# Chunked attention and two expert layers on one core: wider conversion steps, scales finished from PSUM, later maxima

## The chip, the cores and the metric

The kernel runs on one core of one Trainium2 chip. The metric is the device time of one execution in microseconds (us). The kernel before took 1036.71 us, the median of three runs (1036.70, 1036.71 and 1039.64).

A core has TensorE (PE, matmuls; PEld is its weight load), VectorE (DVE), ScalarE (ACT), GpSimd (POOL) and SyncE (SP, which issues the transfers here).

## The reference

Three layers follow each other. All inputs are float32.

- Attention in chunks of 64: 8 batches, 8 heads, 576 positions, head dimension 64. In each chunk `softmax(q k^T / 8) v`. The result is 4608 rows of 512.
- `h = max(x @ w_in, 0)`, then `(h * h) @ w_out`, with w_in 512 x 2048 and w_out 2048 x 512.
- A soft mixture: `logits = x @ phi` (32 slots), one softmax over all 4608 rows, which mixes the rows into 32 slot inputs; eight experts of four slots each (`max(s @ w1, 0) @ w2`); one softmax over the slots, which mixes the slot outputs back into 4608 rows.

w_in and w_out arrive as 8-byte floats and are turned into 4-byte floats on the core.

## The kernel before, in words

The rows are worked in 36 tiles of 128 (two batches, one chunk). Blocks of tiles are one, two and then three tiles each. For each block and each of 16 pieces f of the hidden dimension there is one step: `moe_h` (L752, PE, twelve matmuls), relu with a scale (L776, or L778 on DVE), square (L783, L785), a rounded copy gh (L175) and its remainder gl (L795), and `moe_out` (L813 to L815, PE, three matmuls per tile). All matmuls use parts: a rounded high part and a low part that holds what the rounding lost.

A conversion `conv(f)` makes piece f of both weight matrices. Two loads of 512 KB bring the 8-byte words. ACT takes their upper 16 bits and makes a clamped float of them (`up`, L277). DVE joins exponent and mantissa (`join`) with three instructions per matrix of 128x512: L289, L290, L294. Then DVE takes w_in's absolute maximum (`total`, L169), PE spreads it over the partitions with a matmul against ones (`reduce`, L192), and DVE finishes a power-of-two scale and its inverse in four small instructions, L200, L201, L202 and L205 (`finish`). ACT rounds w_in's piece with that scale (`hi`, L177), DVE makes the remainder (`lo`, L329), ACT or POOL rounds w_out's piece (`whi`, L175 or L184) and POOL makes its remainder (`wlo`, L339).

Attention tiles 0 to 6 are worked in float32 (`attention32`), 7 to 35 in 16-bit parts (`attention`). Both take maxima (L169) and finish scales by the same four small instructions. For a 16-bit tile ACT rounds q and k (L410), DVE makes the remainders (L415, and L430 for v), and a transfer transposes them (L436).

Order. The conversions, tiles 0 to 8 and the steps of the first three blocks form a list. A planner (`list_schedule`) writes it: each operation has engines that can do it, a duration on each, operations that it depends on, and a rank; at each point the planner takes what can start first, and of those that can start within AHEAD of it the one of lowest rank. HOP is the time that it allows from an operation's end to one that depends on it, and SLACK shifts the choice of engine. The list is then issued in exactly this order on all engines. PARTS tells how many f the first blocks do before the next ones start: with (8, 11), blocks 0 and 1 do f 0 to 7 as steps of 128 and of 256 columns, block 2 does f 0 to 10, then blocks 0 and 1 together do f 8 to 15 as steps of 384 columns, and block 2 the rest.

Code behind the list (blocks 3 to 12, the soft mixture) is ordered by the framework, which can move an instruction ahead into the list where its own model of the engines has a hole. The maxima of w_out, 16 instructions that the code issues with the steps of block 3, are such instructions.

Buffers. Conversions have four sets of load buffers, used in turn. The intermediate values of `up` and `join` lie in buffers that tile 8 uses later (qk16 and p16 of even tiles); the first copies of tile 8 wait for the last join.

Of the kernel before, what the change touches and what calls it, by code (L numbers as in the profile page):

```python
# [39 lines left out]
class Op:  # L40
# [8 lines left out]

    def __call__(self):  # L50
        self.fn(self.eng) if self.choose else self.fn()


def cost_of(kind, n):

    return {
        "read": {"act": 0.23 + 0.00088 * n, "dve": 0.08 + 0.00105 * n},
        "scaled": {"act": 0.26 + 0.00092 * n, "dve": 0.08 + 0.00105 * n},
        "copy": {"act": 0.2 + 0.00083 * n, "dve": 0.1 + 0.0007 * n, "pool": 0.2 + 0.0011 * n},
        "two": {"dve": 0.07 + 0.00105 * n, "pool": 0.2 + 0.0021 * n},  # L60
        "square": {
            "act": 0.2 + 0.00083 * n, "dve": 0.07 + 0.00105 * n, "pool": 0.2 + 0.0021 * n,
        },
    }[kind]
# [7 lines left out]
def kernel(  # L72
# [47 lines left out]
    two = const.tile([P, 2], F32, name="two")  # L120
    one, least = two[:1, 0:1], two[:, 1:2]
# [67 lines left out]
    def pow2_scale(am, n):  # L189

        ps = misc()[:, :n]
        pe.matmul(ps, ones, am, start=True, stop=True)  # L192
        return ps

    def pow2_finish(ps, n, tag, bufs, inv=None):
        gm = sm.tile([P, n], F32, tag=tag + "g", name=tag + "g", bufs=2)
# [11 lines left out]
        return s, inv  # L208
# [29 lines left out]
    def conv(f):  # L238
# [30 lines left out]
        def upper(a, eng):  # L269


            h = raws[a].bitcast(I16)[:, 4 : 4 + 2048].rearrange("p (n t) -> p n t", t=4)[:, :, 0]
            v[a] = qk16_b[(N32 + 1) % 2].rearrange("p a n -> p (a n)").bitcast(F32)[
                :, 512 * a : 512 * a + 512
            ]
            if eng == "act":
                act.activation(out=v[a], in_=h, func=ACTF.Relu, scale=2.0 ** 19, bias=least)  # L277
            else:
                (dve if eng == "dve" else pool).tensor_scalar(
                    v[a], h, -LEAST, 2.0 ** 19, ALU.max, ALU.mult  # L280
                )
            v["off", a] = LEAST if eng == "act" else 0.0

        def join(a):


            m = p16_b[(N32 + 1) % 2].rearrange("p a n -> p (a n)").bitcast(F32)
            s, off = 2.0 ** 19, v["off", a]
            dve.tensor_scalar(m, v[a], (14336.0 + off) * s, -2 * off * s, ALU.max, ALU.add)  # L289
# [4 lines left out]
            dve.scalar_tensor_tensor(  # L294
                out=word(a), in0=word(a), scalar=13, in1=m.bitcast(I32),
                op0=ALU.logical_shift_right, op1=ALU.bitwise_or,
            )

        for a in range(2):
            deps = [(("f", x), n) for x in before for n in ("lo", "wlo", "hi", "whi")]  # L300
            ops[f"load{a}"] = Op("dma", 2.4, deps, 0, lambda a=a: load(a))
        for a in range(2):
            last = [(("f", f - 1), f"join{a}")] if f else []
            ops[f"up{a}"] = Op(
                {"act": 0.72, "dve": 0.65, "pool": 1.5}, None, [f"load{a}", *last], 1 + a,
                lambda e, a=a: upper(a, e),
            )
            ops[f"join{a}"] = Op("dve", 1.65, [f"up{a}"], 1 + a, lambda a=a: join(a))
# [62 lines left out]
    def attention(i):  # L371
# [23 lines left out]
        def finish():  # L395
            v["s"], inv = pow2_finish(v["gm"], 3, "a", 5)
            v["iv"] = inv[:, 2:3]
            if not normed:
                pool.tensor_tensor(
                    out=iv2_all[:, i : i + 1], in0=v["iv"], in1=v["iv"], op=ALU.mult  # L400
                )
            v["es"] = sm.tile([P, 1], F32, tag="es", name="es", bufs=4)
            dve.scalar_tensor_tensor(
                out=v["es"], in0=inv[:, 0:1], scalar=scale, in1=inv[:, 1:2],
                op0=ALU.mult, op1=ALU.mult,
            )
# [111 lines left out]
        def xscale():  # L518
            v["xs"], inv = norm_finish(v["xn"], "x", 4, 77 + 127, 127 - 77)
            dve.scalar_tensor_tensor(  # L520
                out=inv, in0=inv, scalar=1.0 / PSH, in1=v["iv"], op0=ALU.mult, op1=ALU.mult
            )
# [32 lines left out]
        ops["finish"] = Op("dve", 0.6, ["reduce"], 1, finish)  # L555
# [5 lines left out]
        conv_end = [(("f", NF - 1), f"join{a}") for a in range(2)] if i == N32 + 1 else []  # L561
# [17 lines left out]
        ops["sums"] = Op("dve", 0.85, ["exp"], 7, sums)  # L579
# [10 lines left out]
        ops["xl"] = Op("dve", 0.6, ["xh"], 12, xl)  # L590
        return ops

    def attention32(i):
# [20 lines left out]
        def finish():  # L614
            v["s"], inv = pow2_finish(v["gm"], 1, "a32", 5)
            pool.tensor_tensor(out=iv2_all[:, i : i + 1], in0=inv, in1=inv, op=ALU.mult)
# [100 lines left out]
        ops["sums"] = Op("dve", 0.85, ["exp"], 4, sums)  # L717
# [99 lines left out]
    def scales16():  # L817


        nonlocal kappa, beta  # L820
        m = sm.tile([P, 2], BF16, tag="m16", name="m16", bufs=1)
        dve.tensor_reduce(out=m[:, 0:1], in_=wi_max, axis=AX.X, op=ALU.max)
        dve.tensor_reduce(out=m[:, 1:2], in_=wo_max, axis=AX.X, op=ALU.max)
        ps = misc()
        norm_scale(ps[:, 0:1], m[:, 0:1])
        pe.matmul(ps[:, 1:2], ones, m[:, 1:2], start=True, stop=True)
# [6 lines left out]
        dve.tensor_scalar_mul(act_w, inv_w, alpha)  # L833
# [365 lines left out]
    pool.memset(ones, 1.0)  # L1199
# [45 lines left out]
    def list_schedule():  # L1245
        free = {"pe": 3.0, "dve": 3.0, "act": 2.5, "pool": 5.0, "dma": 0.7}
# [7 lines left out]
        def add(task, ops, rank):  # L1254
            for x, (n, op) in enumerate(ops.items()):
                me = (task, n)
                deps = [d if isinstance(d, tuple) else (task, d) for d in op.deps]
# [3 lines left out]
                for d in deps:  # L1261
                    if d not in end:
                        missing[me] += 1
                        after.setdefault(d, []).append((me, op, rank + 0.01 * x))
                if not missing[me]:
                    for e in op.on:
                        avail[e][me] = (rank + 0.01 * x, op)
# [64 lines left out]
        while ph < len(left) or left_s or any(avail.values()):  # L1332
# [56 lines left out]
            fin_ = t + op.on[op.eng]  # L1389
            free[op.eng] = fin_  # L1390
# [80 lines left out]
    while t < end or any(x >= t for x in slots):  # L1471
# [232 lines left out]
```

## Time and profile before

| | |
|---|---|
| runs (median of 3) | 1036.71 us |
| the profiled execution | 1034.19 us, span 1032.4 us, mean granted clock of TensorE 0.967 |
| PE busy | 962.5 us, 93% of the span |
| DVE busy | 658.4 us, 64% |
| ACT busy | 546.5 us, 53% |
| POOL busy | 248.9 us, 24% |
| transfers | 112.18 MB, mean 109 GB/s |
| chain that ended last | PE 74%, DVE 12%, DMA 6% |

The span runs from the first to the last instruction; the execution's own time lies a little above it. Busy shares are means over the whole span; what a stretch is bound by has to be read from that stretch. [...] Where a wait has several causes, the profile names the one that came last.

### The profile page before, as it was taken

How to read it: one execution, taken by the hardware profiler on the slowest of the kernel's cores; microseconds unless marked ns; L12 is line 12 of the kernel's file. 1: busy time of each engine (PE TensorE's matmuls, PEld its weight loads, DVE VectorE, ACT ScalarE, POOL GpSimd, SP SyncE). 2: the span in 40 equal slices, each digit the busy share in tenths (PEclk: the TensorE clock that was granted, in tenths of full speed). 3: DMA queues.
4: the chain of work that ended last, by engine and by line, in shares of the span. 5: the costliest groups of instructions: out<-in, count | busy, mean ns of one | idle time of the engine just before them, and what ended most of it. 6: DMA issues, size and time to landing. Idle time of an engine off the chain costs nothing.

```text
span 1032.4 us, 18731 instructions
## 1 busy us (share of the span) xinstructions
PE 962.5 (93%) x7182; PEld 583.8 (57%) x7182; DVE 658.4 (64%) x1469; ACT 546.5 (53%) x1029; POOL 248.9 (24%) x252
## 2 busy tenths in 40 slices
PE   5667998999999999999999999999999999999983
PEld 4555665677666665555555555555555555554442
DVE  6898887746878977667667666566675562123232
ACT  5665765445558665465555555554655644534132
POOL 3463443432313442112122111111121220001100
PEclk8988998999999999999999999999999999999995
DMA  7746352233363374333233334333334451347998
GB/s 158 207 131 205 70 122 93 53 59 74 79 107 62 60 183 105 62 62 62 63 62 73 69 78 84 66 63 63 62 63 63 123 142 33 86 160 223 298 279 240
DMA packets 248618, 112.18 MB, mean 109 GB/s; under 512 B 208080, under 2 KB 241872, under 8 KB 248528
## 3 DMA queue, kind: packets, MB, share of 16 engines
q1 hardware_dynamic: 248528, 110.98, 45.2%
q8 instruction: 56, 0.92, 0.4%
q14 instruction: 34, 0.28, 0.1%
HBM read 78.71 MB, written 9.44 MB: 85 GB/s over the span
## 4 chain that ended last, share of the span: by engine, by line
PE 74%; DVE 12%; DMA 6%; SPq 2%; ACT 2%; issue 2%; POOL 1%; POOLq 0%; DVEq 0%; ACTq 0%
PE hps L752 31%; PE x L815 10%; PE x L813 10%; PE x L814 10%; DVE p L290 2%; PE ehps L1556 2%; PE misc L990 2%; DVE stage L294 2%; PE misc L977 1%; DMA out_dram<-o 1%; DVE p L289 1%; SPq L1627 1%; DMA qkv<-in_k_dram 1%; PE sop L1642 1%; DMA qkv<-in_q_dram 1%
## 5 line engine op out<-in xcount | busy, mean ns | idle before, releaser
L752 PE MATMUL hps<-xb,wi 128*128 128x384 f16 (+2 forms) x2400 | 416.4, 323 | 3.9 <-DVE wi L329 3.9
L752 PEld LDWEIGHTS <-wi 128*128 128x128 f16 x2400 | 225.7, 99 | 173.1 <-issue 27.2
L813 PE MATMUL x<-wo,gh 128*128 128x512 f16 (+1 forms) x576 | 229.1, 398 | 1.9 <-DVE x2sb L878 1.1
L814 PE MATMUL x<-wo,gh 128*128 128x512 f16 (+1 forms) x576 | 223.3, 388 | 0.0
L815 PE MATMUL x<-wo,gl 128*128 128x512 f16 (+1 forms) x576 | 208.5, 390 | 4.2 <-POOL gl L795 2.1
L795 DVE TENSOR_TENSOR gl<-g,gh 128x384 f16<-128x384 f32 (+1 forms) x162 | 99.7, 616 | 110.8 <-ACT gh L175 107.4
L776 ACT ACTIVATE g<-hps,act_w 128x384 f32<-128x384 f32 x128 | 73.9, 578 | 147.0 <-PE hps L752 115.9
L476 POOL TENSOR_TENSOR ex<-ex,rs 128x512 f32<-128x512 f32 x29 | 31.1, 1073 | 383.9 <-DVE rs L473 260.3
L175 ACT ACTIVATE gh<-g 128x384 f16<-128x384 f32 (+3 forms) x196 | 100.0, 511 | 19.5 <-PE x L814 15.8
L783 ACT ACTIVATE g<-g 128x384 f32<-128x384 f32 (+1 forms) x196 | 100.0, 511 | 4.7
L169 DVE TENSOR_REDUCE am<-qkv 128x1 bf16<-128x512 f32 x94 | 63.8, 686 | 48.0 <-DMA qkv<-in_k_dram 20.0
L425 POOL TENSOR_SCALAR vbd<-qkv,as 64x512 f16<-64x512 f32 x58 | 58.6, 1010 | 54.6 <-PE x L815 13.5
L815 PEld LDWEIGHTS <-gl 128*128 128x128 f16 x384 | 37.0, 98 | 44.6 <-DVE gl L795 2.8
L814 PEld LDWEIGHTS <-gh 128*128 128x128 f16 x384 | 37.5, 98 | 36.7 <-issue 1.4
L415 DVE SCALAR_TENSOR_TENSOR qk<-qkv,as,qk 128x512 f16<-128x512 f32 x58 | 54.7, 967 | 5.3 <-ACT qk L410 4.7
L813 PEld LDWEIGHTS <-gh 128*128 128x128 f16 x384 | 37.5, 98 | 36.1 <-issue 0.4
L776 ACT ACTIVATE g<-hps,inv_w 128x384 f32<-128x384 f32 (+1 forms) x70 | 37.5, 537 | 28.8 <-PE hps L752 23.8
L440 DVE COPY qbd<-qkT 64x1024 f16<-64x1024 f16 x58 | 25.6, 441 | 41.5 <-DMA qkT<-qk 41.1
L430 DVE SCALAR_TENSOR_TENSOR vbd<-qkv,as,vbd 64x512 f16<-64x512 f32 x58 | 47.4, 817 | 5.4 <-POOL vbd L425 4.4
L410 ACT ACTIVATE qk<-qkv,as 128x512 f16<-128x512 f32 x58 | 38.5, 712 | 15.8 <-DVE as L202 15.8
L813 PEld LDWEIGHTS x<-wo,gh 128*128 128x128 f32 x192 | 37.1, 193 | 15.9 <-issue 3.7
L795 POOL TENSOR_TENSOR gl<-g,gh 128x384 fp32r<-128x384 f32 (+2 forms) x38 | 36.4, 960 | 35.9 <-ACT gh L175 27.6
(223 smaller groups left out, 1394.1 us busy)
## 6 DMA issues: line engine op xcount, KB each, us to landing
unit<-in_moe_w_dram SPq DMA_DIRECT2D x36, 512.0 KB, 4.2
unit<-in_moe_w_dram SPq DMA_DIRECT2D x56, 256.0 KB, 5.7
qkv<-in_q_dram SPq DMA_DIRECT2D x72, 128.0 KB, 3.4
qkv<-in_k_dram SPq DMA_DIRECT2D x72, 128.0 KB, 3.4
qkv<-in_v_dram SPq DMA_DIRECT2D x72, 128.0 KB, 3.3
stage<-in_moe_w_in_dram SPq DMA_DIRECT2D x16, 512.0 KB, 4.9
stage<-in_moe_w_out_dram SPq DMA_DIRECT2D x16, 512.0 KB, 5.6
out_dram<-o SPq DMA_DIRECT2D x16, 256.0 KB, 4.2
```

The lines of the kernel that those rows point to most:

```text
L169: dve.tensor_reduce(out=am, in_=src, axis=AX.X, op=ALU.max, apply_absolute_value=True)
L175: act.activation(out=out, in_=in_, func=ACTF.Copy)
L415: dve.scalar_tensor_tensor(out=qk16[:, 2 * a + 1], in0=flat[:, a], scalar=v["s"][:, a : a + 1], in1=qk16[:, 2 * a], op0=ALU.mult, op1=ALU. ...
L425: pool.tensor_scalar(out=dst[0], in0=vin, scalar1=v["s"][pr, 2:3], scalar2=1.0, op0=ALU.mult, op1=ALU.mult,)
L430: dve.scalar_tensor_tensor(out=dst[1], in0=vin, scalar=v["s"][pr, 2:3], in1=dst[0], op0=ALU.mult, op1=ALU.subtract,)
L752: pe.matmul(hp, wi[f][:, wl, kt], xb[:, xl, kt, :n], start=(nm == 0), stop=(nm == 3 * KT - 1))
L776: act.activation(out=r["g"], in_=r["hp"], func=ACTF.Relu, scale=sc)
L783: act.activation(out=g, in_=g, func=ACTF.Square)
L795: (dve if eng == "dve" else pool).tensor_tensor(out=r["gl"], in0=r["g"], in1=r["gh"] if parts16(b) else r["gh"].bitcast(F32), op=ALU.subtract,
L813: pe.matmul(o, gh[:, c], w[:, 0], start=first, stop=False)
L814: pe.matmul(o, gh[:, c], w[:, 1], start=False, stop=False)
L815: pe.matmul(o, gl[:, c], w[:, 0], start=False, stop=last)
```

## The change

- `up` runs on ACT only, and writes both matrices into one buffer of 128x1024. `join` becomes one operation: L289's and L290's instructions run once over 1024 columns, L294's stays one per matrix. It waits for both loads. The buffers are now qk16 of both tile parities, so the first copies of tiles 7 and 8 both wait for the last join.
- `pow2_scale` gets a second matmul that adds a tiny constant, and the ones become 2^-13. `pow2_finish` then needs two instructions, both reading PSUM, and no lower bound. The powers of two that this shifts are made good where the scales are used.
- The maxima of w_out become an operation `wmax` of the list. It depends on the last join, and its rank is raised by 200.
- PARTS goes from (8, 11) to (9, 12). The planner has new durations, ranks, HOP, AHEAD and SLACK. A new `share` lengthens some DVE operations in the plan when POOL is busy.

```diff
-PARTS = (8, 11)
+PARTS = (9, 12)
-AHEAD = 0.01
-HOP = 0.15
-SLACK = {'act': 3.5, 'dve': -2.69, 'pool': -0.65}
+AHEAD = 0.2
+HOP = 0.18
+LATER = 200.0
+SLACK = {'act': 0.39, 'dve': -3.6, 'pool': -0.9}
...
-        pe.matmul(ps, ones, am, start=True, stop=True)
+        pe.matmul(ps, ones, am, start=True, stop=False)
+        pe.matmul(ps, ones, tiny[:, :n], start=False, stop=True)
...
-        dve.tensor_scalar_max(gm, ps, 2.0 ** -100)
-        dve.tensor_single_scalar(gm.bitcast(I32), gm.bitcast(I32), 0x7F800000, ALU.bitwise_and)
+        bits = ps.bitcast(I32)
         dve.tensor_scalar(
-            s.bitcast(I32), gm.bitcast(I32), -1.0, float(268 << 23), ALU.mult, ALU.add
+            s.bitcast(I32), bits, 0x7F800000, 0x7F800000, ALU.bitwise_xor, ALU.bitwise_and
         )
-        dve.tensor_scalar(
-            inv.bitcast(I32), gm.bitcast(I32), float(-(14 << 23)), None, ALU.add
-        )
+        dve.tensor_single_scalar(inv.bitcast(I32), bits, 0x7F800000, ALU.bitwise_and)
...
+        def join():
+            u, m, s, off = wide(0), wide(1), 2.0 ** 19, LEAST
+            dve.tensor_scalar(m, u, (14336.0 + off) * s, -2 * off * s, ALU.max, ALU.add)
+            dve.scalar_tensor_tensor(
+                out=m.bitcast(I32), in0=u, scalar=(off - 14336.0) * s, in1=m,
+                op0=ALU.min, op1=ALU.add,
+            )
+            for a in range(2):
+                dve.scalar_tensor_tensor(
+                    out=word(a), in0=word(a), scalar=13,
+                    in1=m.bitcast(I32)[:, 512 * a : 512 * a + 512],
+                    op0=ALU.logical_shift_right, op1=ALU.bitwise_or,
                 )
...
+        last = [(("f", f - 1), "join")] if f else []
         for a in range(2):
+            ops[f"up{a}"] = Op("act", 0.67, [f"load{a}", *last], 1, lambda a=a: upper(a))
+        ops["join"] = Op("dve", 3.3, ["up0", "up1"], 2, join)
...
+        ops["wmax"] = Op(
+            "dve", 0.61, ["whi", (("f", NF - 1), "join")], 6,
+            lambda: largest_of(wo[f][:, 0].bitcast(F32), wo_max[:, f : f + 1]),
+        )
...
-        conv_end = [(("f", NF - 1), f"join{a}") for a in range(2)] if i == N32 + 1 else []
+        conv_end = [(("f", NF - 1), "join")] if i in (N32, N32 + 1) else []
...
+            if op.eng == "dve" and op.share:
+                fin_ += op.share * min(1.0, max(0.0, free["pool"] - t) / op.on["dve"])
...
-            if b == F16_FROM - 2:
-                largest_of(wo[f][:, 0].bitcast(F32), wo_max[:, f : f + 1])
```

The ranks of tiles and conversions (RANK_T, RANK_F, RANK_S), the cost table and the single durations are replaced by new numbers throughout.

## Rows read from the trace of the kernel before

**Rows 1.** Busy us by stretch: PE, PEld, DVE, ACT, POOL; then clock, DMA share, GB/s

```profile
18.00:100.00 82.00, 58.45 (x644) 45.41 (x643) 76.16 (x168) 51.34 (x96) 39.31 (x46) 0.87 0.61 167
100.00:180.00 80.00, 73.27 (x381) 49.61 (x380) 64.84 (x119) 50.46 (x96) 32.57 (x31) 0.95 0.43 105
180.00:232.00 52.00, 52.00 (x380) 36.76 (x379) 32.25 (x58) 25.03 (x46) 18.89 (x19) 1.00 0.30 55
...
340.00:940.00 600.00, 596.20 (x4279) 335.44 (x4278) 365.23 (x858) 320.92 (x603) 113.93 (x100) 1.00 0.38 84
```

**Rows 2.** PE's waits, 18 to 100 us: us in total, times, longest

```profile
PE misc L192 <- DVE wi_max L169: 5.6, 5, 1.7
PE misc L676 <- POOL ex L669: 3.9, 3, 1.9
PE hps L752 <- DVE wi L329: 3.9, 4, 2.2
PE misc L192 <- DVE wg L200: 3.5, 2, 2.9
```

**Rows 3.** PE's waits, 100 to 180 us

```profile
PE misc L192 <- DVE wi_max L169: 6.2, 3, 3.8
```

**Rows 4.** DVE's timeline at 42.66 us: start, us, line, operation

```profile
42.66 0.15 DVE L200 TENSOR_SCALAR wg<-misc 128x1 f32<-128x1 f32 x1
...
43.03 0.15 DVE L202 TENSOR_SCALAR ws<-wg 128x1 int32<-128x1 int32 x1
...
43.16 0.74 DVE L698 SCALAR_TENSOR_TENSOR xb<-misc,a32s,xb 128x512 f16<-128x512 f32 x1
```

**Rows 5.** L200 by stretch: length, DVE busy and count

```profile
18.00:100.00 82.00, 2.07 (x14) 0.87 0.61 167
100.00:180.00 80.00, 1.20 (x8) 0.95 0.43 105
```

**Rows 6.** The maxima of w_out by stretch

```profile
18.00:100.00 82.00, 4.73 (x7) 0.87 0.61 167
100.00:180.00 80.00, 5.45 (x8) 0.95 0.43 105
```

**Rows 7.** L294 by stretch

```profile
18.00:100.00 82.00, 11.67 (x15) 0.87 0.61 167
100.00:180.00 80.00, 11.70 (x16) 0.95 0.43 105
180.00:232.00 52.00, 0.69 (x1) 1.00 0.30 55
```

**Rows 8.** PE's timeline at 346 us

```profile
346.14 0.18 PE L192 MATMUL misc<-am,ones 128*128 128x3 bf16 x1
346.18 4.06 PE L752 MATMUL hps<-xb,wi 128*128 128x384 f16 x24
```

**Rows 9.** The h matmuls by shape, 0 to 330 us: count, busy us, mean ns

```profile
L752 PE MATMUL hps<-xb,wi 128*128 128x384 f16 x576 | 103.2, 331 | 0.0
...
L752 PE MATMUL hps<-xb,wi 128*128 128x256 f16 x96 | 14.4, 311 | 0.0
...
L752 PE MATMUL hps<-xb,wi 128*128 128x128 f16 x96 | 8.2, 234 | 3.9 <-DVE wi L329 3.9
```

**Rows 10.** POOL's and DVE's timelines at 164 us

```profile
164.07 1.17 POOL L795 TENSOR_TENSOR gl<-g,gh 128x384 fp32r<-128x384 f32 x1 [0.38 <-POOL gl L795]
...
164.42 1.37 DVE L290 SCALAR_TENSOR_TENSOR p<-qk,p 128x512 int32<-128x512 f32 x1
...
168.14 0.69 DVE L290 SCALAR_TENSOR_TENSOR p<-qk,p 128x512 int32<-128x512 f32 x1
```

**Rows 11.** L415 of tiles 7 and later, by shape, 0 to 330 us

```profile
L415 DVE SCALAR_TENSOR_TENSOR qk<-qkv,as,qk 128x512 f16<-128x512 f32 x16 | 15.5, 986 | 0.6 <-ACT qk L410 0.5
```

**Rows 12.** Transfers by kind, 0 to 260 us: count, us to landing

```profile
qkT<-qk SPq DMA_TRANSPOSE x4, 5.2
```

**Rows 13.** DVE's timeline at 219 us

```profile
219.49 0.69 DVE L534 SCALAR_TENSOR_TENSOR xb<-misc,xb 128x512 f16<-128x512 f32 x1 [4.29 <-ACT xb L528]
```

More of the change, by code (lines that the diff above doesn't have):

```diff
@@ L48, in __init__ @@
         self.deps, self.stage, self.fn = deps, stage, fn
+        self.share = 0.0
     def __call__(self):
@@ L56, in cost_of @@
     return {
[L57 to L60, printed above, removed]
+        "read": {"act": 0.13 + 0.00092 * n, "dve": 0.08 + 0.00105 * n},
+        "scaled": {"act": 0.27 + 0.00088 * n, "dve": 0.08 + 0.00105 * n},
+        "copy": {"act": 0.12 + 0.0008 * n, "dve": 0.1 + 0.0007 * n, "pool": 0.2 + 0.0013 * n},
+        "two": {"dve": 0.07 + 0.00105 * n, "pool": 0.2 + 0.0023 * n},
         "square": {
-            "act": 0.2 + 0.00083 * n, "dve": 0.07 + 0.00105 * n, "pool": 0.2 + 0.0021 * n,
+            "act": 0.2 + 0.0009 * n, "dve": 0.07 + 0.00105 * n, "pool": 0.2 + 0.0024 * n,
         },
@@ L119 @@
     ones = const.tile([P, P], BF16, name="ones")
-    two = const.tile([P, 2], F32, name="two")
-    one, least = two[:1, 0:1], two[:, 1:2]
+    four = const.tile([P, 4], F32, name="four")
+    one, least, tiny = four[:1, 0:1], four[:, 1:2], four[:, 2:4].bitcast(BF16)
     phi_sb = const.tile([P, KT, NS], F32, name="phi_sb")
@@ L187, in copy, with pow2_scale @@
             )
-    def pow2_scale(am, n):
-        ps = misc()[:, :n]
-        pe.matmul(ps, ones, am, start=True, stop=True)
+    def pow2_scale(am, n, ps=None):
+        ps = misc()[:, :n] if ps is None else ps
+        pe.matmul(ps, ones, am, start=True, stop=False)
+        pe.matmul(ps, ones, tiny[:, :n], start=False, stop=True)
         return ps
     def pow2_finish(ps, n, tag, bufs, inv=None):
-        gm = sm.tile([P, n], F32, tag=tag + "g", name=tag + "g", bufs=2)
         s = sm.tile([P, n], F32, tag=tag + "s", name=tag + "s", bufs=bufs)
@@ L267, in load, with wide, upper @@
             )
-        def upper(a, eng):
+        def wide(x):
+            return qk16_b[x].rearrange("p a n -> p (a n)").bitcast(F32)
+        def upper(a):
             h = raws[a].bitcast(I16)[:, 4 : 4 + 2048].rearrange("p (n t) -> p n t", t=4)[:, :, 0]
[L273 to L280, printed above, removed]
-                )
[L282 to L289, printed above, removed]
+            act.activation(
+                out=wide(0)[:, 512 * a : 512 * a + 512], in_=h, func=ACTF.Relu,
+                scale=2.0 ** 19, bias=least,
+            )
+        def join():
+            u, m, s, off = wide(0), wide(1), 2.0 ** 19, LEAST
+            dve.tensor_scalar(m, u, (14336.0 + off) * s, -2 * off * s, ALU.max, ALU.add)
             dve.scalar_tensor_tensor(
-                out=m.bitcast(I32), in0=v[a], scalar=(off - 14336.0) * s, in1=m,
+                out=m.bitcast(I32), in0=u, scalar=(off - 14336.0) * s, in1=m,
                 op0=ALU.min, op1=ALU.add,
             )
[L294 to L297, printed above, removed]
+            for a in range(2):
[4 more added lines that the diff above has]
+                )
         for a in range(2):
@@ L590, in attention @@
         ops["xl"] = Op("dve", 0.6, ["xh"], 12, xl)
+        for n in ("lo0", "lo1", "vl0", "vl1", "qd0", "qd1", "normal"):
+            ops[n].share = 0.4
         return ops
@@ L825, in scales16 @@
         norm_scale(ps[:, 0:1], m[:, 0:1])
-        pe.matmul(ps[:, 1:2], ones, m[:, 1:2], start=True, stop=True)
+        pow2_scale(m[:, 1:2], 1, ps[:, 1:2])
         alpha, inv_alpha = norm_finish(ps[:, 0:1], "n16", 1, 55 + 127, 127 - 55)
@@ L1256, in add @@
                 me = (task, n)
+                r = rank + 0.01 * x + later.get(n, 0.0)
                 deps = [d if isinstance(d, tuple) else (task, d) for d in op.deps]
@@ L1263, in add @@
                         missing[me] += 1
-                        after.setdefault(d, []).append((me, op, rank + 0.01 * x))
+                        after.setdefault(d, []).append((me, op, r))
                 if not missing[me]:
                     for e in op.on:
-                        avail[e][me] = (rank + 0.01 * x, op)
+                        avail[e][me] = (r, op)
         def finished(me):
```

63 lines of the change are left out of this document (34 added, 29 removed).

## The prediction

> **What bounds the kernel now.** I read the busy time by stretches first, then what PE waited for, then single stretches of VectorE's timeline. From 340 to 940 us PE is busy 596.20 of 600 us at full clock: there nothing that DVE saves can shorten the run, and every matmul that is added lengthens it [rows 1]. The same holds from 180 to 232 us, PE 52.00 of 52. Before that it is different. [...] So the only time to be won is some 30 us of PE idle, and in the first stretch DVE is the engine that is full. The waits say the same: 5.6 us for the reduction of wi_max, 3.9 for the low half of wi, 3.5 for wg, all DVE, against 3.9 for POOL's normalization [rows 2]; from 100 to 180 us 6.2 of the 6.73 us are the wait for wi_max [rows 3].
>
> **The change part by part.** DVE work is counted by how far starts lie apart, not by the printed duration, since neighbours overlap.
>
> Scales from PSUM (B). The four instructions of a scale start at 42.66 us and the next one at 43.16: 0.50 us, of which the last two, which don't wait for each other, take 0.13 [rows 4]. The change keeps two that both read PSUM: 0.13, if a PSUM operand costs what it costs L200, 0.15 us like its SBUF neighbours. Saved 0.37. Ends: 0 (if each still waited for the other's full length) and 0.50. From 18 to 100 us there are 14 scales, from 100 to 180 us 8 [rows 5]: 5.2 and 3.0 us of DVE.
>
> w_out's maxima (A). In the code they stand far behind the list, but the trace has 7 of them in 18 to 100 us and 8 in 100 to 180 us [rows 6]: they went into holes that were expected in DVE's order, where DVE is in truth full. Each is one instruction, with no transfer, busy 0.68 us and takes some 0.6 from its neighbours. Now they are in the list behind the last join: 4.2 and 4.8 us leave the two stretches. They land in 180 to 232 us, where DVE is busy 32.25 of 52 [rows 1]; 15 times 0.6 more is 9.0, which leaves room, so I cost them at nothing there; what hides them is PE's work of those 52 us. If that cover is gone, see the third rival.
>
> 1024-wide steps (C). An instruction that waits for the one before costs about 0.18 us beyond its elements, one that doesn't 0.07 (0.37 for the first two of rows 4, 0.13 for the last two). Merging two matrices saves one L289 (0.07 to 0.18), one L290 (0.18), and lets the second L294 start without waiting (0.12): 0.36 to 0.48, taken as 0.4 per pair. 15 L294 lie in 18 to 100 us and 16 in 100 to 180 us [rows 7], so 7.5 and 8 pairs: 3.0 and 3.2 us. Ends: 0 (a pair is no faster) and 0.48. [...]
>
> What the merge adds is a wait: the join now needs both loads and both ACT conversions, where w_in's half went ahead alone before. Behind it on DVE's queue stand the total, the scale and the low half, and PE's h step waits for that. The order is written anew around it, and other DVE work stands between; each of 16 conversions has some 10 us, since their joins go from 18 to behind 180 us today [rows 7]. Cost 0, at most the 3.9 us that PE waits for wi in rows 2, once more.
>
> Sum on DVE: 12.4 us in 18 to 100 us, 11.0 us in 100 to 180 us. How much of it PE gets: in the first stretch 13.0 of the 23.55 idle us are put down to DVE by name, 0.55, and DVE is 93% busy; between 0.55 and 1 I take 0.65, nearer the row: 8.1 us (ends 6.8 and 12.4). In the second PE has only 6.2 us of such waits; I take half, 3.1 (ends 0 and 6.2).
>
> The clock. With fewer holes PE is granted more: 58.45 us at 0.87 would be 4.9 us less at the 0.95 of the next stretch. I take 1.0 of 0 to 4.9.
>
> The second matmul of each scale. At full speed the matmul behind L192 starts 0.04 us after it [rows 8]. Some 28 scales lie behind 180 us (the last conversion's and one for each of tiles 9 to 35), where PE is full: 1.1 us more; the other end is the matmul's own 0.18 us, 5.0. Those before 180 us hide in PE's idle time.
>
> PARTS. One f more is done as 128 and 256 columns instead of 384: 12 matmuls of 8.2/96 and 14.4/96 us for 12 of 103.2/576 [rows 9], 12 times 0.056 = 0.7 us in a stretch where PE idles. Cost 0, at most 0.7. The planner's new durations, hop and ranks are no work; what they may do is in the rivals.
>
> Sum: -8.1 - 3.1 - 1.0 + 1.1 = -11.1 us. The profiled execution took 1034.19 us (span 1032.4), so 1023.1; the median of the runs, 1036.71, lies 2.5 above it: **1025.6 us**. With all ends to the good (B 0.50, C 0.48, a share of 1) it is -14.8 - 6.2 - 4.9 + 1.1 = -24.8, 1012; with all to the bad (B and C 0, so 4.2 times 0.55) -2.3 + 5.0 + 0.7 + 3.9 = +7.3, 1044, which needs five mishaps at once.
>
> **The rivals.**
> 1. The gain goes to POOL's shared path. At 164.07 us POOL starts a gl of 1.17 us, and the L290 that DVE starts at 164.42 takes 1.37 us, against 0.69 for one that meets nothing at 168.14 [rows 10]. An instruction twice as wide blocks POOL, or is blocked, longer. If each of the 32 wide L289 and L290 puts off a POOL instruction by a further 0.35 us, that is 11.2 us on POOL, and PE waits for POOL already (3.9 us in rows 2). All of it on PE's path: 1025.6 + 11.2 = 1036.8, no change. For: the stretched row. Against: POOL is busy 39.31 of 82 us, and fewer, longer instructions also meet less often. [...] Chance 0.10.
> 2. PE's idle time is only named after DVE and ends next at something else: the loads (DMA busy 0.61 of 18 to 100 us) or ACT (51.34 of 82). Then the gain is 3.2 to 5 us, 1031.7 to 1033.5. For: the remaining 10.5 us of idle have other names. Against: no transfer leads the waits. Chance 0.08.
> 3. Slower: the first f16 tiles come late. Both wide buffers of the join are now the q and k buffers of tiles 7 and 8, so the first copies of tile 7 too wait for the last join, which lies behind 180 us today [rows 7]. These copies are ACT's, and if ACT stands before them, the relu of the next step stands behind them, and PE with it. Behind it, DVE would have 9.0 us of maxima and tile 7's two subtractions of 0.99 us [rows 11], and SP's queue tile 7's transpose of 5.2 us ahead of tile 8's [rows 12]: 9.0 + 2.0 + 5.2 = 16.2 us. Tile 8's last instruction ends at 220.2 us [rows 13], and PE, full until then, goes on to the next block that needs it. If all that falls ahead of tile 8, PE idles 16.2 us: 1025.6 + 16.2 = 1041.8. It decides from 14.2 us of lateness (11.1 plus 3.1 for 0.3%). Against: the maxima have the lowest rank, the transposes of the two tiles overlap DVE work, and the last join itself comes earlier. Chance 0.14.
>
> **How the numbers follow.** Forecast, a gain of 5 to 25 us: 0.66. Rival 2: 0.08. Rival 1: 0.10. Rival 3: 0.14. More than 25 us: 0.02. About 0.3% of this kernel, 3 us, can be told from no change. Faster holds the forecast, rival 2 and the last: 0.76; same is rival 1: 0.10; slower is rival 3: 0.14. The range goes from 1012, where the good ends meet, to 1039, above rival 1 and short of rival 3.
>
> **What would show it.** Right: no maxima of wo before the last L294; two DVE instructions per scale about 0.07 us apart; L289 near 0.7 us and L290 near 1.25 us where POOL is still; PE idle in 18 to 100 us down from 23.55 to about 15, and the next block's first h near 210 instead of 220 us; from 340 us on nothing shorter. Wrong: DVE less busy in 18 to 100 us and PE's idle time as before (rival 2), POOL's gl longer and named in PE's waits (rival 1), or PE idle just before the block that follows the list, waiting for xb (rival 3).

## The result, and the profile after

The changed kernel took 1027.31 us in the median of four runs (1026.07 to 1028.71), the kernel before 1037.69 us beside it (1036.7 to 1039.64). The ratio is 0.9901, with a 95% interval of 0.9882 to 0.9921: 10.3 us gained, where the sum said 11.1. The profiled execution took 1028.09 us (span 1026.4, mean granted clock 0.978).

The busy time by stretches of the kernel after, with the columns of [rows 1]:

```profile
18.00:100.00 82.00, 62.32 (x709) 49.10 (x708) 74.64 (x124) 59.04 (x115) 53.52 (x56) 0.96 0.72 197
100.00:180.00 80.00, 76.53 (x483) 52.91 (x483) 61.60 (x100) 48.19 (x88) 38.86 (x33) 1.00 0.29 81
180.00:232.00 52.00, 46.95 (x311) 32.77 (x310) 33.12 (x56) 21.45 (x39) 19.22 (x20) 0.93 0.31 65
340.00:940.00 600.00, 594.93 (x4286) 333.95 (x4287) 351.80 (x797) 316.11 (x597) 112.08 (x96) 1.00 0.38 87
```

Against [rows 1] PE idles 19.68 us instead of 23.55 in the first stretch and 3.47 instead of 6.73 in the second. The granted clock, a share of full speed, rose from 0.87 to 0.96 and from 0.95 to 1.00. Busy time multiplied by the clock is an estimate of how much work was done, since in before twelve h matmuls of 128x384 took 4.00 us at a clock of 0.50 (from 161.14 us on), where 24 took 4.06 us at 1.00 [rows 8]: 59.8 against 50.9 in the first stretch, 76.5 against 69.6 in the second. Then something is given back: from 180 to 232 us, where PE had been busy for all 52.00 us, it now idles 5.05 us at a clock of 0.93, and does 43.7 against 52. By this estimate the net of the three stretches is some 7.5 us.

A lead is easy to follow at one recurring instruction: ACT's copy of a finished block out of PSUM (x2sb, L880 before, L893 after; for the last block L177 and L180), called a *store* below. ACT's timeline has it here, first before, then after (start, length, line, operation):

```profile
170.84 0.67 ACT L880 ACTIVATE x2sb<-x,iv_all 128x512 f32<-128x512 f32 x1
```

```profile
163.99 0.68 ACT L893 ACTIVATE x2sb<-x,iv_all 128x512 f32<-128x512 f32 x1
```

That is a lead of 6.8 us near 170 us. The stores near 304, 383 and 945 us of before lead by 8.3, 11.4 and 7.6 us, and the span by 6.0. The two profiled executions are thus closer to each other than the medians of the runs, which are 10.4 us apart.

What PE waited for in 18 to 232 us after (us in total, times, longest):

```profile
PE misc L195 <- DVE wi_max L172: 7.8, 7, 1.7
PE misc L459 <- DVE qbd L448: 4.8, 1, 4.8
PE x L827 <- POOL gl L807: 3.5, 4, 2.3
```

The waits for wi_max were 5.6 and 6.2 us in the two stretches of before [rows 2, 3] and are 7.8 together, and the one for wg [rows 2] is gone. The second row, PE's wait for the spread copy of q of a 16-bit tile (qbd), is new: most of what the third stretch lost. DVE's timeline after shows each part of the change, and where w_out's maxima went:

```profile
22.14 0.15 DVE L205 TENSOR_SCALAR a32s<-misc 128x1 int32<-128x1 int32 x1
22.20 0.15 DVE L208 TENSOR_SCALAR a32i<-misc 128x1 int32<-128x1 int32 x1
22.76 0.69 DVE L292 TENSOR_SCALAR qk<-qk 128x1024 f32<-128x1024 f32 x1 [0.41 <-ACT qk L283]
23.49 1.23 DVE L293 SCALAR_TENSOR_TENSOR qk<-qk,qk 128x1024 int32<-128x1024 f32 x1
24.75 1.30 DVE L298 SCALAR_TENSOR_TENSOR stage<-stage,qk 128x512 int32<-128x512 int32 x2
25.96 0.68 DVE L660 TENSOR_REDUCE mx<-misc 128x8 f32<-128x512 f32 x1
...
158.10 2.46 DVE L172 TENSOR_REDUCE wo_max<-wo 128x1 bf16<-128x512 f32 x4
...
164.42 2.46 DVE L172 TENSOR_REDUCE wo_max<-wo 128x1 bf16<-128x512 f32 x4
...
167.45 1.40 DVE L423 SCALAR_TENSOR_TENSOR qk<-qkv,as,qk 128x512 f16<-128x512 f32 x2
...
170.32 2.47 DVE L172 TENSOR_REDUCE wo_max<-wo 128x1 bf16<-128x512 f32 x4
...
179.82 0.69 DVE L172 TENSOR_REDUCE am<-qkv 128x1 bf16<-128x512 f32 x1 [2.16 <-DMA qkv<-in_v_dram]
...
183.36 2.91 DVE L423 SCALAR_TENSOR_TENSOR qk<-qkv,as,qk 128x512 f16<-128x512 f32 x2
...
190.80 2.08 DVE L448 COPY qbd<-qkT 64x1024 f16<-64x1024 f16 x2 [1.32 <-DMA qkT<-qk]
```

Two instructions finish a scale 0.06 us apart, and the wide L292 and L293 take 0.69 and 1.23 us. The last join ends at 158 us and no longer behind 180, and the maxima start right behind it: 16 of them between 158.1 and 172.8 us, twelve ahead of the two remainders (L423) of the first 16-bit tile, 7. Tile 8's two follow at 183.36 us.

### The profile page after: what moved, and what is told of

Same layout as the page of the kernel before. It is cut to its first block, busy times and chain, and to the rows that moved or that the text cites. A ratio compares the mean times of both kernels' runs of the same rounds, so it can differ in the third digit from the quotient of the medians.

```text
span 1026.4 us, 18712 instructions
## 1 busy us (share of the span) xinstructions
PE 958.2 (93%) x7247; PEld 581.6 (57%) x7247; DVE 639.5 (62%) x1330; ACT 542.7 (53%) x1023; POOL 273.2 (27%) x265
## 4 chain that ended last, share of the span: by engine, by line
PE 69%; DVE 12%; DMA 7%; SPq 3%; ACT 3%; POOL 3%; issue 2%; DVEq 0%; POOLq 0%; ACTq 0%
PE hps L764 28%; PE x L827 10%; PE x L825 10%; PE x L826 10%; DMA qkv<-in_k_dram 2%; DVE stage L298 2%; PE ehps L1572 2%; DVE qk L293 1%; DMA qkT<-qk 1%; DMA out_dram<-o 1%; PE misc L1003 1%; PE misc L990 1%; SPq L1643 1%; DMA unit<-in_moe_w_dram 1%; DVE qk L292 1%
## 5 line engine op out<-in xcount | busy, mean ns | idle before, releaser
L764 PE MATMUL hps<-xb,wi 128*128 128x384 f16 (+2 forms) x2412 | 411.3, 320 | 3.3 <-DVE wi L331 2.7
L795 ACT ACTIVATE g<-g 128x384 f32<-128x384 f32 (+2 forms) x196 | 99.8, 509 | 4.9
L433 POOL TENSOR_SCALAR vbd<-qkv,as 64x512 f16<-64x512 f32 x58 | 62.1, 1070 | 51.3 <-DVE ai L208 39.3
L438 DVE SCALAR_TENSOR_TENSOR vbd<-qkv,as,vbd 64x512 f16<-64x512 f32 x58 | 54.9, 946 | 6.4 <-POOL vbd L433 4.7
L423 DVE SCALAR_TENSOR_TENSOR qk<-qkv,as,qk 128x512 f16<-128x512 f32 x58 | 57.9, 1006 | 1.3 <-ACT qk L418 0.5
L807 POOL TENSOR_TENSOR gl<-g,gh 128x384 fp32r<-128x384 f32 (+2 forms) x39 | 42.6, 1094 | 39.7 <-ACT gh L178 31.6
L827 PEld LDWEIGHTS x<-wo,gl 128*128 128x128 f32 x192 | 35.8, 190 | 16.4 <-POOL gl L807 5.6
L497 POOL TENSOR_TENSOR p<-ex,p 128x512 f16<-128x512 f32 x29 | 40.7, 1404 | 9.8 <-ACT p L494 8.4
```

The lines of the kernel that those rows point to most:

```text
L423: dve.scalar_tensor_tensor(out=qk16[:, 2 * a + 1], in0=flat[:, a], scalar=v["s"][:, a : a + 1], in1=qk16[:, 2 * a], op0=ALU.mult, op1=ALU. ...
L433: pool.tensor_scalar(out=dst[0], in0=vin, scalar1=v["s"][pr, 2:3], scalar2=1.0, op0=ALU.mult, op1=ALU.mult,)
L438: dve.scalar_tensor_tensor(out=dst[1], in0=vin, scalar=v["s"][pr, 2:3], in1=dst[0], op0=ALU.mult, op1=ALU.subtract,)
L764: pe.matmul(hp, wi[f][:, wl, kt], xb[:, xl, kt, :n], start=(nm == 0), stop=(nm == 3 * KT - 1))
L795: act.activation(out=g, in_=g, func=ACTF.Square)
L807: (dve if eng == "dve" else pool).tensor_tensor(out=r["gl"], in0=r["g"], in1=r["gh"] if parts16(b) else r["gh"].bitcast(F32), op=ALU.subtract,
```

## The experiments

Theories tested: **A, B, C** are the prediction's parts, each with its own worth, and against them stand rival 3 (tiles 7 and 8 come late), and the view that the written order itself is the change. The table gives before, after and the twelve experiments, each against the runs of before beside it, and the stores near 171, 304 and 383 us of before (us). The stores are those of one profiled execution each, which can lie some us from the median.

| kernel | median us | ratio | 95% | stores |
|---|---|---|---|---|
| before | 1037.7 | | | 170.8, 303.8, 383.3 |
| after | 1027.3 | 0.9901 | 0.9882 to 0.9921 | 164.0, 295.5, 371.9 |
| e_narrow | 1031.4 | 0.9944 | 0.9924 to 0.9965 | 168.8, 295.5, 370.9 |
| e_four_ops | 1030.6 | 0.9934 | 0.9915 to 0.9953 | 168.1, 298.8, 377.4 |
| e_wmax_behind | 1023.9 | 0.9864 | 0.9842 to 0.9886 | 161.8, 289.4, 365.8 |
| e_old_plan | 1048.4 | 1.0109 | 1.0084 to 1.0135 | 157.1, 315.3, 392.4 |
| e_wmax_tail | 1027.2 | 0.9895 | 0.9872 to 0.9917 | 158.8, 287.1, 371.9 |
| b_wmax_later | 1043.6 | 1.0062 | 1.0041 to 1.0083 | 167.8, 311.6, 389.6 |
| b_two_ops | 1032.0 | 0.9939 | 0.9916 to 0.9963 | 164.3, 297.9, 373.8 |
| e_old_behind | 1044.1 | 1.0057 | 1.0037 to 1.0076 | 158.2, 314.0, 389.1 |
| b_bar7 | 1036.5 | 0.9980 | 0.9966 to 0.9993 | 169.7, 304.6, 383.8 |
| e_T | 1030.4 | 0.9916 | 0.9888 to 0.9944 | 164.0, 293.9, 371.4 |
| e_parts | 1027.5 | 0.9898 | 0.9879 to 0.9918 | 159.8, 295.0, 372.0 |
| e_behind_one | 1022.7 | 0.9851 | 0.9830 to 0.9872 | 163.1, 288.4, 369.5 |

### One part of the change undone

**e_narrow** is the kernel after with its two wide join instructions cut into halves, in the same order:

```
+            for a in range(2):
+                c = slice(512 * a, 512 * a + 512)
-            dve.tensor_scalar(m, u, ...)
-            dve.scalar_tensor_tensor(out=m.bitcast(I32), in0=u, ...)
+                dve.tensor_scalar(m[:, c], u[:, c], ...)
+                dve.scalar_tensor_tensor(out=m.bitcast(I32)[:, c], in0=u[:, c], ...)
```

> The changed kernel with its order kept instruction for instruction, only the two 1024-wide join instructions each split into two of 512. Theory D (the gain is DVE time freed in the first 180 us, by the sizes of the prediction): 3.0 of 12.4 us of DVE come back before 100 us and 3.2 of 11.0 after, so the time is 2.9 us above the changed kernel (ratio to before 0.993). Rival P (the gain is the new order and its ranks; how long DVE takes for a join is hidden): under 1 us above it (0.990 to 0.991). Rival W (the wide instructions lose to POOL what they save): no slower than the changed kernel, or faster by 1 to 3 us.

Its ratio is 0.0043 above that of after: 4.5 us are lost, in the median of twelve runs that lie from 1028.06 to 1037.28. The intervals just don't overlap, the runs do. DVE's timeline of it, at the conversion that the fence above shows at 22.76 us, and PE's largest wait in 18 to 232 us:

```profile
22.59 0.42 DVE L294 TENSOR_SCALAR qk<-qk 128x512 f32<-128x512 f32 x1
...
26.17 0.68 DVE L663 TENSOR_REDUCE mx<-misc 128x8 f32<-128x512 f32 x1
```

```profile
PE misc L195 <- DVE wi_max L172: 13.5, 9, 2.0
```

A pair takes 3.58 us from start to the next instruction, the merged one 3.20: 0.38 us saved, within the 0.36 to 0.48 that was worked out. The wait that a slower join lengthens, PE's for wi_max, went from 7.8 to 13.5 us. So C saves DVE's time, and the runs show that it is worth something. How the 4.5 us come about isn't shown by this trace: the profiled execution took 1028.54 us, 0.5 more than that of after, PE idles 2.83 instead of 5.05 us from 180 to 232 us, and from the store at 295.5 us on it isn't behind.

**e_four_ops** puts two small instructions back into each scale:

```
+        gm = sm.tile([P, n], F32, ...)
+        dve.tensor_scalar_max(gm, ps, 2.0 ** -120)
+        dve.tensor_single_scalar(gm..., gm..., 0x7F800000, ALU.bitwise_and)
-        bits = ps.bitcast(I32)
+        bits = gm.bitcast(I32)
```

> The changed kernel with two more small DVE instructions per scale (a maximum from PSUM and a mask), so four as before, in the same places of the list. Theory D: 0.37 us for each of 22 scales before 180 us, 5.2 of 12.4 and 3.0 of 11.0 us of DVE, so 4.2 us above the changed kernel (ratio to before 0.994). Rival P: under 1 us above it.

3.4 us are lost: the runs (1029.84 to 1031.68) lie above all of after's, though the intervals overlap a little. DVE's timeline of it:

```profile
44.78 0.14 DVE L205 TENSOR_SCALAR wg<-misc 128x1 f32<-128x1 f32 x1
44.96 0.15 DVE L206 TENSOR_SCALAR wg<-wg 128x1 int32<-128x1 int32 x1
45.15 0.15 DVE L208 TENSOR_SCALAR ws<-wg 128x1 int32<-128x1 int32 x1
45.22 0.14 DVE L211 TENSOR_SCALAR inv_w<-wg 128x1 int32<-128x1 int32 x1
45.28 0.68 DVE L172 TENSOR_REDUCE wi_max<-stage 128x1 bf16<-128x512 f32 x1
```

0.50 us a scale, 0.18 for each instruction that waits and 0.07 for each that doesn't, as in [rows 4]. The two that stayed cost about the same with a PSUM operand: 0.14 us after (44.18 to 44.32 us), 0.13 here with one from SBUF (45.15 to 45.28). B is real too, and b_two_ops below shows it alone.

**e_wmax_behind** takes w_out's maxima out of the list, so that they are issued with the steps of block 3 as before:

```
-        ops["wmax"] = Op("dve", 0.61, ["whi", (("f", NF - 1), "join")], 6, ...)
...
+            if b == F16_FROM - 2:
+                largest_of(wo[f][:, 0].bitcast(F32), wo_max[:, f : f + 1])
```

> The changed kernel with the 16 maxima of w_out taken out of the list and issued with the steps of block 3 as before, from where the framework moves them ahead into the list again. Theory D: 4.2 of 12.4 and 4.8 of 11.0 us of DVE, so 4.1 us above the changed kernel (0.994), with maxima before 100 us in the trace. Rival P: under 1 us above it. If the maxima behind the last join are what makes tiles 7 and 8 late at 186 us (PE waits 4.8 us for a copy of q there), that wait gets shorter by some of the 10 us of maxima between 158 and 172 us.

The sign is wrong: it is 3.8 us *faster* than after; the runs of the two don't overlap (at most 1025.23 here, at least 1026.07 there), though the intervals overlap a little. The maxima lie spread from 28.0 to 162.9 us, much as in before (24.3 to 184.2). Its stretch from 180 to 232 us is full again, at full clock:

```profile
180.00:232.00 52.00, 51.94 (x354) 36.53 (x353) 33.29 (x60) 26.14 (x48) 21.21 (x22) 1.00 0.46 84
```

A path for it can be read on SP's queue. First the kernel after, then e_wmax_behind (L423 after is L419 here), each with the transposing transfers of tiles 7 and 8 and, between them, loads of tile 9 (those of tiles 7 and 8 are issued by 105 us in both):

```profile
169.66 2.90 SPq L444 DMA_TRANSPOSE qkT<-qk  x1
172.61 1.30 SPq L377 DMA_DIRECT2D qkv<-in_k_dram  x2
...
186.33 2.79 SPq L444 DMA_TRANSPOSE qkT<-qk  x1
```

```profile
166.08 2.97 SPq L440 DMA_TRANSPOSE qkT<-qk  x1
169.10 1.29 SPq L373 DMA_DIRECT2D qkv<-in_k_dram  x2
...
183.68 2.98 SPq L440 DMA_TRANSPOSE qkT<-qk  x1
```

DVE's remainders of tile 7 in e_wmax_behind:

```profile
163.72 0.90 DVE L419 SCALAR_TENSOR_TENSOR qk<-qkv,as,qk 128x512 f16<-128x512 f32 x1
```

They start at 163.72 us there and at 167.45 in after, behind the maxima: 3.7 us. The transposing transfer needs them and starts 3.6 us later; tile 9's loads of k and v stand behind it on SP's queue, 3.5 us later. On DVE tile 9's maxima (am) run ahead of tile 8's remainders, and in after DVE waits 2.16 us for v there (179.82 us above). Tile 8's remainders start at 183.36 us, in e_wmax_behind at 181.45; its transpose follows 2.7 us later than there, and its scores are the matmuls that PE waits 4.77 us for, as PE's timeline after has it (in e_wmax_behind they start at 189.65 us, and PE is busy until then):

```profile
192.94 0.23 PE L459 MATMUL misc<-qkT,qbd 128*128 128x64 f16 x1 [4.77 <-DVE qbd L448]
```

**e_parts** sets `PARTS = (8, 11)` in the kernel after.

> The changed kernel with PARTS (8, 11) as before, all else of its plan kept. The prediction costs PARTS at nothing: within 1 us of the changed kernel, 0.989 to 0.991. Theory L: with (8, 11) the last stretch of the list holds 5 steps of block 2 instead of 4, some 4 us more cover for tiles 7 and 8, so the 4.8 us wait gets shorter, 0.986 to 0.988. Rival P (ranks and PARTS fit only each other): 3 us or more slower than the changed kernel, over 0.993.

1027.54 us, the same as after: the 0.7 us costed at nothing are nothing. But the idle time lies elsewhere. The wait for qbd is gone, and PE is busy 50.98 of the 52 us from 180 to 232; instead it is busy only 72.00 of the 80 us from 100 to 180 (76.53 in after), and waits for a copy of a finished block that stands behind five maxima on DVE. DVE's timeline and PE's:

```profile
160.97 3.05 DVE L172 TENSOR_REDUCE wo_max<-wo 128x1 bf16<-128x512 f32 x5
```

```profile
164.73 0.79 PE L825 MATMUL x<-wo,gh 128*128 128x512 f32 x1 [3.15 <-DVE x2sb L891]
```

So the 4.77 us wait of after can go without the time getting shorter.

### One part alone, on the kernel before

**b_two_ops** gives the kernel before the two-instruction scales and the second matmul, in before's order.

> The kernel before with this one edit: two DVE instructions per scale instead of four, and the second matmul; the list is unchanged. Theory D (freed DVE time): 22 scales before 180 us, 0.37 us each, 4.2 us faster less 1.1 us of matmuls, ratio 0.997. Rival P (only the planned order counts): 0.999 to 1.001.

6.3 us were won, twice what was expected (3.1). By stretches, of an execution that took 1026.78 us, the fastest of the six and 5.2 under their median:

```profile
18.00:100.00 82.00, 61.88 (x685) 49.24 (x684) 72.51 (x140) 52.41 (x101) 39.63 (x47) 0.86 0.64 174
180.00:232.00 52.00, 52.00 (x405) 36.73 (x404) 32.34 (x58) 24.30 (x45) 17.88 (x19) 1.00 0.30 62
```

PE idles 20.12 instead of 23.55 us in the first, at the old clock, and keeps its full 52.00 us in the third: what B wins in front isn't given back.

**b_wmax_later** gives it the maxima behind the last join, with the lowest rank:

```
+        ops["wmax"] = Op("dve", 0.61,
+            ["whi", (("f", NF - 1), "join0"), (("f", NF - 1), "join1")], 6, ...)
...
-            if b == F16_FROM - 2:
-                largest_of(wo[f][:, 0].bitcast(F32), wo_max[:, f : f + 1])
```

> The kernel before with this one edit: the maxima of w_out in the list, behind the last join, rank raised by 200. Theory A: 13 of 16 maxima leave full stretches of DVE, 4.1 us faster, ratio 0.996. Theories H and L: nothing gained in front, and the maxima stand before tile 8's work, 0 to 5 us slower, 1.000 to 1.005, with PE waiting near 190 us.

6.4 us *slower* than before. The store near 171 us comes 3.1 us earlier, so DVE's relief in front is real; the next comes 7.8 us later. By stretch, DVE's timeline, and PE's largest wait of that stretch:

```profile
180.00:232.00 52.00, 47.54 (x348) 32.66 (x348) 36.24 (x66) 24.80 (x44) 19.43 (x19) 0.97 0.30 55
```

```profile
183.51 7.80 DVE L169 TENSOR_REDUCE wo_max<-wo 128x1 bf16<-128x512 f32 x13
```

```profile
PE misc L507 <- DMA pT<-p: 3.4, 1, 3.4
```

Thirteen maxima stand in one piece of 7.80 us on DVE, and PE idles 4.46 us of a stretch in which it had idled none.

### The order

**e_old_plan** has the operations of after under before's planner numbers (`AHEAD`, `HOP`, `SLACK`, ranks, the cost table, `PARTS`, and no `share`; the single durations stay those of after); **e_old_behind** the same with the maxima issued as before:

```
-PARTS = (9, 12)
-AHEAD = 0.2
-HOP = 0.18
-RANK_T = [-144.12, -188.54, ...]
+PARTS = (8, 11)
+AHEAD = 0.01
+HOP = 0.15
+RANK_T = [-239.64, -159.73, ...]
...
```

> The changed kernel's operations, planned with the numbers of before: PARTS (8, 11), AHEAD, HOP, SLACK, all ranks, the cost table, and no share. Theory D: DVE work is as small as in the changed kernel, so most of the gain stays: 0 to 4 us above the changed kernel (0.990 to 0.994). Rival P: the gain is gone, 10 us above it (0.998 to 1.003).

> The changed kernel's operations under the old plan numbers (1048.35 us, ratio 1.011, PE idle 14.8 us from 180 to 232 us), and the maxima issued with block 3 as before. Theory L: the 10 us of maxima that stand at 182 to 204 us before tiles 7 and 8 leave, and 5 to 10 us of the idle time go, 1038 to 1043 us, ratio 1.001 to 1.006. Rival: the old ranks alone make the tiles late, since both now wait for the last join; no more than 2 us change, 1.009 to 1.013.

e_old_plan is 1.09% *slower than before*. Its early store is the earliest of all (157.1 us), its next one 11.5 us behind before's. Its stretch from 180 to 232 us and PE's largest wait in it:

```profile
180.00:232.00 52.00, 37.23 (x277) 25.09 (x276) 37.50 (x65) 18.71 (x32) 18.89 (x19) 0.91 0.32 56
```

```profile
PE misc L511 <- DMA pT<-p: 6.5, 1, 6.5
```

PE idles 14.77 us, almost the 16.2 us of rival 3, and waits for attention tiles. Without the maxima (e_old_behind) 5.4 us come back and PE is busy 42.34 us, still 9.66 short. So the maxima are a part of the lateness, and the larger part is something else in the old order. One candidate can be seen: tile 7's first copies, which now wait for the last join. In before ACT makes them at 140.65 us, in e_old_behind 0.6 us behind the end of the join (ACT's timeline before; DVE's and ACT's of e_old_behind):

```profile
140.65 1.32 ACT L410 ACTIVATE qk<-qkv,as 128x512 f16<-128x512 f32 x2
```

```profile
181.53 1.98 DVE L298 SCALAR_TENSOR_TENSOR stage<-stage,qk 128x512 int32<-128x512 int32 x2
184.12 1.32 ACT L414 ACTIVATE qk<-qkv,as 128x512 f16<-128x512 f32 x2
```

Tile 7's transposing transfer then starts at 187.54 us, where before had it at 144.70. Ranks that don't fit and this wait weren't separated.

**e_wmax_tail** is after with the maxima behind tile 8's loads (`["whi", (("t", 8), "xl")]` for the dependence on the last join).

> The changed kernel with the maxima of w_out still in the list but behind the last instruction of tile 8. Its list is that of the kernel with the maxima issued with block 3 (1023.87 us, ratio 0.986), only that the maxima are not in front. Theory A (the prediction's: a maximum in front takes 0.6 us from a full DVE, 4.1 us of time in all): 4.1 us faster than that kernel, ratio 0.982. Theory H (the framework puts them into stretches where DVE waits anyway): within 1 us of it, 0.985 to 0.987. Both expect the wait of 4.8 us for tile 8's copy of q to be gone (theory L: the maxima between 158 and 172 us and the order planned around them make tiles 7 and 8 late).

0.9895, no better than after, in runs from 1023.86 to 1029.41 us; the trace is that of the slowest. The wait for tile 8's copy of q is gone, as both theories expected. Up to the store of 287.1 us it leads e_wmax_behind by 2.3 us; at the next, 371.9, it is 6.1 us behind. Between them, its stretch from 300 to 320 us, where after has 19.68 us of PE and a clock of 1.00, and PE's timeline:

```profile
300.00:320.00 20.00, 16.67 (x127) 10.10 (x124) 14.67 (x29) 13.28 (x24) 7.86 (x7) 0.83 0.36 57
```

```profile
214.74 0.50 PE L827 MATMUL x<-wo,gl 128*128 128x512 f32 x1 [2.05 <-DVE gl L807]
...
309.67 0.80 PE L764 MATMUL hps<-xb,wi 128*128 128x384 f16 x2 [3.05 <-DVE xg L227]
```

A wait of 3.05 us and the lower clock account for some of it. Why that wait arose wasn't settled, nor whether the faster runs have it. The first of the two waits is again one behind maxima: they now stand at 202.55 us (twelve, 7.20 us) and at 211.64 us (four, 2.46 us) on DVE, and the gl that PE waits for starts behind the last of them.

**b_bar7** makes tile 7's first copies of the kernel before wait for a join as well (`conv_end = [(("f", 14), "join1")]`: conversion 14's; for the last one, 15, the planner finds no order).

> The kernel before with this one edit: the first copies of tile 7 wait for the join of conversion 14 (at some 170 us), where they stand at 140 us now; for the last join itself the plan of before has no order. Theory bar (the wait that the wide buffers put on tile 7 is a part of what the change gives back): PE idles for tiles 7 or 8 between 180 and 232 us, where it is busy 52.00 of 52 now, and the time is 2 us or more above before, ratio over 1.002. Rival: tile 7 has time enough until block 3, under 1 us, 0.999 to 1.001.

0.998, and PE busy 50.95 of the 52 us: with conversion 14, whose copies of tile 7 start at 171.95 us, the wait costs nothing. For the last conversion it wasn't tried on before.

**e_T** tells the planner that q and k's transpose takes 4.2 instead of 1.8 us; from issue to landing it took 5.2 us before [rows 12] and, up to 260 us, 4.7 us after, both medians.

> The changed kernel with one planner duration changed: a transpose of q and k is planned with 4.2 us instead of 1.8 (the trace shows 5.2 us from issue to landing). Theory T (the 4.8 us wait of PE for tile 8's copy of q is a transpose planned too short): the wait goes, 3 to 5 us faster than the changed kernel, ratio 0.985 to 0.987. Theory L (the maxima at 158 to 172 us are in the way, however the transpose is planned): the wait is only moved, within 1.5 us of the changed kernel, 0.989 to 0.992.

The wait for qbd is gone, the time stays (0.9916, runs from 1025.99 to 1034.55 us). PE's timeline has the next one in its place:

```profile
204.96 0.20 PE L511 MATMUL misc<-pT,vbd 128*128 128x64 f16 x1 [2.82 <-DMA pT<-p]
```

**e_behind_one** is e_wmax_behind without the second matmul of a scale (`pe.matmul(ps, ones, am, start=True, stop=True)` alone).

> The fastest kernel so far (the changed kernel with the maxima issued with block 3, ratio 0.986) without the second matmul of each scale; the list is the same otherwise. By the prediction's 0.04 us for each of 28 scales behind 180 us: 1.1 us faster, ratio 0.985. By the growth of a steady block between the two profiles (0.3 us per block of three tiles, 10 blocks): 3 us faster, 0.983. Rival: the matmul hides and nothing changes, 0.986 to 0.987.

1022.74 us, ratio 0.9851: the fastest version, 1.5% under before and below the interval of after. Against e_wmax_behind the 1.3 us agree with the 1.1 costed, but the intervals overlap. From the store near 450 us to the last one the times are 487.6 us before, 489.4 after and 488.4 here.

## Why the prediction came out, and where it didn't

The total was right, 10.3 us for 11.1. Not all of its steps were.

- **Bound.** Right. From 340 us on nothing got shorter: PE's idle time from 340 to 940 us went from 3.80 to 5.07 us, and the lead at the stores shrank from 11.4 us near 383 to 7.6 near 945. What was won was won ahead of 340 us, by the estimate some 3 us of it from 320 to 340 us, where PE was busy 17.64 us at a clock of 0.93 before and 19.41 at 1.00 after.
- **Share.** The row read as 13.0 of 23.55 idle us for DVE left out 2.8 us of smaller waits for DVE from 18 to 100 us (wi_max 0.9, ex 1.2, xb 0.4, am 0.3), which rival 2 counted among the 10.5 us that "have other names". With them the share is 0.67, near the 0.65 that was taken.
- **B, scales.** The 0.37 us a scale are right: 0.50 us with four instructions, 0.13 expected with two (0.14 after, from 44.18 to 44.32 us). By the shares of the sum it was worth 4.2 us, or 3.1 with the second matmul; measured were 3.4 by undoing it, and 6.3 alone on before, twice the term. Why it was worth more alone stays open.
- **C, wide steps.** Right in size on DVE, 0.38 us a pair for 0.4; worth 4.5 us by undoing it (an estimate of its range from the two intervals is 1.5 to 7.4), where its share of the sum was some 2.9 (3.0 times 0.65 and 3.2 times 0.28).
- **A, maxima.** Wrong. The step failed at "I cost them at nothing there; what hides them is PE's work of those 52 us". The relief in front was right in sign (3.1 and 3.0 us at the first store, alone on before and by e_wmax_tail against e_wmax_behind). But the maxima stand in a row on an engine that the attention tiles need, and PE's full 52.00 us rested on those tiles being on time: 6.4 us lost alone, 3.8 us within the change. That the two runs lose by the maxima's place is shown; the path over SP's queue within the change is read from two traces. Other plans (e_parts, e_T, e_wmax_tail) lose the wait for qbd and not the time; in e_parts and e_wmax_tail another wait stands behind maxima in its place. That the maxima landed at 158 and not at 180 us, since the join itself came earlier, wasn't in the sum, though rival 3 names the earlier join.
- **The order.** "The planner's new durations, hop and ranks are no work" was true and no reason for a price of nothing. The same operations took 1.0109 under the old numbers and 0.9901 under the new ones: 21.6 us, twice the whole sum. This difference is no gain that could be added, since the old order also meets the new wait of tile 7: what the new ranks alone are worth on the old operations wasn't run. The parts undone one by one give 3.4 + 4.5 - 3.8 = 4.1 of the 10.3 us; the other 6.2 can't be put down to one of them. A alone came out 7.9 us below its share of the sum (4.2 times 0.65 and 4.8 times 0.28, the shares taken, are 4.1; measured -3.8), so the agreement of the total is partly luck: what A missed, the rest made up.
- **Clock.** 1.0 us was too little: 0.87 to 0.96 in the first stretch. PE idles 19.68 us there, not the 15 that was to be seen, and still does some 9 us more of work: 3.87 us more busy at 0.96 are 3.7, and 58.45 us at a clock 0.09 higher are 5.3. This splits the estimate and doesn't show what the clock alone is worth. The premise, fewer holes and more clock, is the order of three stretches in [rows 1] (23.55 idle us at 0.87, 6.73 at 0.95, none at 1.00) and isn't borne out over the runs: from 18 to 100 us PE idles 20.12 us at 0.86 in b_two_ops, 17.38 us at 0.90 in e_wmax_behind and 19.68 us at 0.96 in after.
- **Second matmul and PARTS.** Second matmul: about 1 us, not resolved. PARTS: nothing, as costed.
- **Rival 1** (POOL). POOL's busy time rose from 248.9 to 273.2 us, but PE's waits for POOL's gl and ex in the first stretch fell from 5.5 us (1.6 and 3.9) to 3.8 (2.6 and 1.2). POOL's gl of 128x384 got longer, as this rival had it, from 1.08 to 1.21 us in the mean up to 330 us. In [rows 10] the L290 beside POOL's gl takes 1.37 us and ends 0.55 us after the gl, less than the 0.69 us of a quiet one: it shows a delay, and no more than that. The wide instructions weren't stretched much more than the narrow ones: L293 and L292 took 0.23 and 0.32 us more in the mean than at 22.76 us, L290 and L289 of before 0.25 and 0.23 us more than their shortest shown. This rival didn't decide the time.
- **Rival 3** happened to a third: 5.05 us of idle for 16.2. Its maxima ahead of the tiles and its transposes on SP's queue are what the rows show. The wait of tile 7's copies, with which it began, had no cost with conversion 14 (b_bar7). In after the copies start at 159.20 us, 1.0 us behind the end of the last join, and under the old plan at 184.12 us, where PE idles most; what it costs there wasn't separated.

## What to carry to other kernels

Work that is moved from a full engine into a hole has to be costed by what stands behind it in its new place, over the queues that it puts off (here DVE, then SP's transfers, then DVE again and PE), and not by whether the engine has room on average. Where an order is written out by hand or by a planner, changed operations and their order are one change: price the order by running the new operations in the old one. An agreement of the total says little on the parts; undo each alone.

## What the runs showed of the hardware

- Small VectorE instructions on 128x1: those that read what the one before wrote started 0.18 and 0.19 us behind it (e_four_ops, 44.78, 44.96 and 45.15 us). One that doesn't started 0.07 us behind with its operand in SBUF (e_four_ops, 45.15 and 45.22 us), and 0.06 and 0.07 us behind with it in PSUM (after, 22.14 and 22.20 us, 44.18 and 44.25 us).
- Two matmuls of 128x3 in a row cost PE less than their printed 0.17 and 0.16 us: PE's timeline after in the steady part has the second 0.02 us behind the first and the next work 0.03 us behind that.

```profile
506.35 0.17 PE L195 MATMUL misc<-am,ones 128*128 128x3 bf16 x1
506.37 0.16 PE L196 MATMUL misc<-four,ones 128*128 128x3 bf16 x1
506.40 3.25 PE L764 MATMUL hps<-xb,wi 128*128 128x384 f16 x19
```

- The wide instructions took longer in the mean than their shortest. By form, up to 330 us after (count, busy us, mean ns):

```profile
L293 DVE SCALAR_TENSOR_TENSOR qk<-qk,qk 128x1024 int32<-128x1024 f32 x16 | 23.3, 1457 | 0.6
L292 DVE TENSOR_SCALAR qk<-qk 128x1024 f32<-128x1024 f32 x16 | 16.2, 1010 | 3.6 <-ACT qk L283 3.5
```

At 22.76 us the same two took 1.23 and 0.69. The narrow ones of before were stretched too: L290 took 0.94 us in the mean and 0.69 at its shortest shown, L289 0.65 and 0.42. What stretched them in each case wasn't separated.
